# Scratch in DRAM in rows of 2304 and 3072 bytes instead of 6144 to 12288

## Chip, cores and metric

One core of a Trainium2 chip runs the whole kernel. The metric is the device time of one launch in microseconds (us). Everything is float32; matmuls of the FFN use float32r operands, split into a high and a low part.

## What is computed

A block of an adaLN-conditioned model on x of 2048 x 576: a state-space convolution (S4D) in the first half, a ReLU FFN of width 4608 in the second, each behind a layernorm that is scaled and shifted by a conditioning vector.

```python
mod = (_silu(c) @ w_mod).reshape(c.shape[0], 6, 1, -1)
sa, ca, ga, sb, cb, gb = (mod[:, i] for i in range(6))
h = _layernorm(x) * (1 + ca) + sa
# A_ref: K = 2 Re(sum_n C exp(A dt pos)), 576 channels x 2048 taps, with a diagonal A of 128 modes
#        y = irfft(rfft(h) * rfft(K)) causal, by channel;  + h * D_skip
x = x + ga * _A_ref(h, ...)
h = _layernorm(x) * (1 + cb) + sb
x = x + gb * (maximum(h @ w1, 0) @ w2)      # w1 576 x 4608, w2 4608 x 576
```

## The kernel before

The 2048 rows are cut into four blocks of 512 (NB). A block's convolution gives its x2 and the transposed h for the FFN; the FFN of a block takes 36 steps (NF), one for each 128 columns of w1.

**Before the FFN.** The class `KGen` computes the convolution's taps as products of factors: `W2` (2 x 32 per channel) and `W1` (16 x 2 per channel), 128 modes on the partitions, in six groups of 96 channels. For the first block the products are made at once (L71 in a helper). The factors are needed again for the other blocks' taps, so `sines` stores W2 (L328), and `save` W1 (L342), to DRAM tiles `W2d` and `W1d`, through SP's queue. One partition's line is 12288 B in W2d and 6144 B in W1d, contiguous in SBUF and in DRAM.

**The FFN** (`ffn`) runs over g = 0..143, 36 steps a block. A step loads w1 and w2 (tiles `r`), ScalarE rounds them to the high part `w` (L1246, L1256). In block 0, VectorE also computes the low part (L1249, L1259, L1260), and SP stores it to `L1d` and `L2d` (L1348); in the other three blocks SP loads it back (L1239, L1263) instead. `first` makes 14 matmuls into `hps` (L1273), `second` 14 into `acc` (L1299). The w tiles have two buffers, so a load is issued when the matmuls two steps back are done. All these transfers, about 1.2 MB a step in lines of 2304 and 2560 B, go through SP's hardware queue (q1).

**Beside the FFN** of block s runs a generator (`gens`) that prepares block s + 1. `step` draws from it at fixed points of the loop. In block 0 it is `rest` (taps of the later blocks from W1d, Zd and W2d: loads at L449 to L451, rotations on VectorE at L459 to L465, small matmuls at L490, stores `kd` at L431) and then `conv(1)`; in block 1 `finish(0)`, the remaining taps and `conv(2)`; in block 2 `finish(1)` and `conv(3)`; in block 3 `finish(2)`. The convolution works on spectra of 4 x 2 x 288 numbers for each of 128 frequencies: U of h, K of the taps, R of the taps before the split. `save` (L806) and `load` (L802) keep them in DRAM tiles `Ud`, `Kd`, `Rd`, one line of 9216 B for each partition; `product` (L972) loads a K and a U for each earlier block and multiplies them on VectorE (L994 to L1000). `conv` also loads its block of x (L909), again in lines of 9216 B. All these transfers go through POOL's software queue (q0).

The Tile framework orders instructions within an engine at build time and places the waits; what `keep_in_program_order` (class `Kept`) marks stays as written. Each engine runs its instructions in order.

Of the kernel before, what the change touches and what calls it, by code (L numbers as in the profile page):

```python
# [10 lines left out]
F32 = mybir.dt.float32  # L11
# [7 lines left out]
P = 128  # L19
# [8 lines left out]
H = 48  # L28
NH = 12
PC = 288  # L30
# [19 lines left out]
class KGen:  # L50
# [256 lines left out]
    def first(self, setup, mod):  # L307

        nc, k = self.nc, self.k
        self.W1, self.Z, self.E, self.F = {}, {}, {}, {}
        W2s, ke, ps = {}, None, {}

        def sines(g):
            E, F = self.E.pop(g), self.F.pop(g)
            W2 = W2s[g] = [
                self.pw.tile([P, 2, 32, H], F32, tag="W2", bufs=5, name=f"W2_{2 * g + u}")
                for u in range(2)  # L320
            ]
            ends = self.half_values(g, W2, E[2:4], F[0], True)
            yield
            self.half_values(g, W2, E[0:2], F[1], False)
            for out, a, b, op in ends:
                self.v(out, a, b, op)
            for u in range(2):
                nc.sync.dma_start(out=k.W2d[2 * g + u], in_=W2[u].rearrange("p r b c -> p (r b c)"))  # L328
            self.moduli = self.powers(g, E[4], F[2])
            zs = self.Z[g][1]  # L330
            for u in range(2):
                nc.sync.dma_start(out=k.Zd[2 * g + u], in_=zs[:, :, :, u * H : u * H + H])

        def rows(g):
            qs = slice(24 * (g % 3), 24 * (g % 3) + 24)
            self.act(ke[:, :, qs], ps[g].rearrange("p q a -> p a q"), AF.Copy)
            if g % 3 == 2:
                self.store(0, g // 3, ke.rearrange("p a q -> p (a q)"), nc.sync)

        def save(g):  # L340
            for u in range(2):
                nc.sync.dma_start(  # L342
                    out=k.W1d[2 * g + u], in_=self.W1[g][:, u].rearrange("p a r c -> p (a r c)")
                )

        def end():
            save(NG - 1)
            rows(NG - 1)

        def run(*gens):  # L350
            for x in gens:
                for _ in x:
                    pass

        def some(x, n):
            for _ in range(n):
                next(x, None)

        next(setup)
        next(mod)  # L360
        early = k.early(self)
        next(early)
        turns = self.turns(0)
        next(turns)
        next(setup)
        some(turns, 2)
        next(setup)
        run(turns, self.exps(0))
        next(mod)
        next(setup)  # L370
        next(mod)
        values = sines(0)
        next(values)
        next(mod)
        run(values)
        late = iter(())
        for g in range(NG):
            self.moduli()
            if g + 1 == NG:
                next(early)  # L380
            double = [
                self.doubling(g, i, u)
                for i, u in (
                    (0, slice(0, 2)), (1, slice(0, 2)), (2, slice(0, 1)), (2, slice(1, 2)),
                    (3, slice(0, 1)), (3, slice(1, 2)),
                )
            ]
            if g + 1 < NG:
                for i, _ in enumerate(self.exps(g + 1)):
                    some(late, 2 - i % 2)  # L390
            run(*double[:2])
            next(mod, None)
            run(double[2])
            if 0 < g < 5:
                next(early)
            if g + 1 < NG:
                turns = self.turns(g + 1)
                for _ in range(2):
                    next(turns)
                    some(late, 2)  # L400
                next(double[3])
                next(turns)
                run(late, turns, double[3])
            else:
                run(late, double[3])
            if g + 1 == NG:
                next(early)
            if g > 0:
                rows(g - 1)
            run(*double[4:])  # L410
            if g + 1 < NG:
                save(g)
            if g % 3 == 0:
                ke = self.pc.tile([P, 16, 72], F32, tag="ke", bufs=1, name=f"ke_{g}")
            ps[g] = self.ps.tile([P, 512], F32, tag="kps", name=f"kps_{g}")[:, :384].rearrange(
                "p (q a) -> p q a", a=16
            )
            a, late = (self.products(ps[g], self.W1[g], W2s[g][u], u) for u in range(2))
            if g + 2 == NG:
                self.kt0 = self.pw.tile([P, 16, 72], F32, tag="W2", bufs=5, name="kt_0")  # L420
                k.load_kt(self.kt0, 0, 0, nc.sync)
            if g + 1 < NG:
                run(a, sines(g + 1))
            if g + 2 == NG:
                next(early)
        return a, late, end
# [8 lines left out]
    def rest(self, psum, hs, blocks):  # L435


        nc, k = self.nc, self.k
        v = nc.vector.tensor_tensor
        na = 16 * len(blocks)  # L440
        with ExitStack() as ctx:
            pt = k.pool(ctx, f"kr{hs[0]}{blocks[0]}", side="right")

            def load(h):
                W2 = pt.tile([P, 2, 32, H], F32, tag="W2", bufs=2, name=f"W2r_{h}")
                W0 = pt.tile([P, 16, 2, H], F32, tag="W0", bufs=2, name=f"W0_{h}")
                Z = pt.tile([P, 2, 2, H], F32, tag="Z", bufs=2, name=f"Zr_{h}")
                d = nc.gpsimd.dma_start
                d(out=W0.rearrange("p a r c -> p (a r c)"), in_=k.W1d[h])  # L449
                d(out=Z.rearrange("p i r c -> p (i r c)"), in_=k.Zd[h])  # L450
                d(out=W2.rearrange("p r b c -> p (r b c)"), in_=k.W2d[h])  # L451
                return W2, W0, Z

            def rot(out, X, Z, i):
# [60 lines left out]
            for h in hs:  # L515
                W2, W0, Z = nxt
# [5 lines left out]
            yield from prev  # L522


def spread(a, b, n):

    for i, w in enumerate(a):
        yield w
        if i % n == n - 1:
            yield next(b, 0.0)  # L530
    yield from b


class Body:
# [3 lines left out]
    def build(self):  # L538
        nc, tc, I = self.nc, self.tc, self.I
        with ExitStack() as ctx:  # L540
            dr = ctx.enter_context(tc.tile_pool(name="dram", bufs=1, space=DRAM))
            self.kd = [[dr.tile([P, 16 * 72], F32, name=f"kd_{s}_{p}") for p in range(2)] for s in range(NB)]
            self.W2d = [dr.tile([P, 64 * H], F32, name=f"W2d_{h}") for h in range(NH)]
            self.W1d = [dr.tile([P, 32 * H], F32, name=f"W1d_{h}") for h in range(NH)]
            self.Zd = [dr.tile([P, 4 * H], F32, name=f"Zd_{h}") for h in range(NH)]
            spec = lambda n, m: [
                [dr.tile([P, 8 * PC], F32, name=f"{n}_{i}_{p}") for p in range(2)] for i in range(m)
            ]
            self.Ud, self.Rd, self.Kd = spec("Ud", 4), spec("Rd", 3), spec("Kd", 3)
            self.md = {n: dr.tile([1, D], F32, name=f"md_{n}") for n in ("ca", "sa", "gb")}  # L550
            self.cst = ctx.enter_context(tc.tile_pool(name="cst", bufs=1))
            self.L1d = [dr.tile([P, 640], F32, name=f"L1d_{f}") for f in range(NF)]
            self.L2d = [dr.tile([P, D], F32, name=f"L2d_{f}") for f in range(NF)]
            self.consts()
            self.x2, self.xT, self.ended = {}, {}, -1
            self.dsk = self.cst.tile([1, D], F32, name="dsk")
            nc.gpsimd.dma_start(out=self.dsk, in_=I["dsk"].unsqueeze(0))
            self.sm = self.pool(ctx, "sm")
            self.x2p = [self.pool(ctx, "x2a")]
            kg = KGen(self)  # L560
            with ExitStack() as c2:
                kg.open(c2)
                setup = kg.setup(I)
                hooks = dict(zip(("first", "late", "rows"), kg.first(setup, self.mod(kg))))
            self.main(ctx, kg, hooks)
# [233 lines left out]

    def load(self, src, name):  # L800
        t = self.spec(name)
        self.nc.gpsimd.dma_start(out=t.rearrange("p a b c -> p (a b c)"), in_=src)  # L802
        return t

    def save(self, dst, t, eng=None):
        (eng or self.nc.gpsimd).dma_start(out=dst, in_=t.rearrange("p a b c -> p (a b c)"))  # L806

    def transform(self, src, fc, Z, kept=False):

# [91 lines left out]
    def conv(self, s):  # L901

        nc = self.nc
        v = self.vec.tensor_tensor
        xp = self.xp[s % 2]
        if s:
            x2 = self.x2p[s % 2].tile([P, 4, D], F32, tag="x2", bufs=1, name=f"x2_{s}")
            self.x2[s] = x2
            nc.gpsimd.dma_start(  # L909
                out=x2,  # L910
                in_=self.I["x"][s * 512 : (s + 1) * 512, :].rearrange("(m n) d -> m n d", n=4),
            )
        else:
            x2, h = self.x2[0], self.h0
            self.fcKn, self.gcn = (
# [579 lines left out]
```

## Time and profile before

| | |
|---|---|
| median of 3 runs | 1414.14 us (1412.53 to 1420.44) |
| the profiled execution | 1418.65 us, span 1416.8 us |
| mean granted TensorE clock | 0.938 |
| TensorE matmul / weight load busy | 1263.9 us (89%) / 996.0 us (70%) |
| VectorE / ScalarE / GpSimd busy | 891.7 us (63%) / 495.4 us (35%) / 180.1 us (13%) |
| q1, SP's queue | 102260 packets, 222.09 MB, 47.9% of 16 engines |
| q0, POOL's queue | 17952 packets, 123.08 MB, 22.9% of 16 engines |
| first FFN matmul of the four blocks | near 229, 610, 913 and 1175 us |

"Busy" is the time in which an engine executes; the ends of matmuls are modelled, so a matmul that waits can look long. The chain of waits is followed back from the last instruction, at each step to what released it. A packet is what one of 16 DMA engines moves at a time; the DMA view gives packets, bytes and engine share by queue, and for each kind of transfer the time from issue to landing.

### The profile page before, as it was taken

The numbers are of one execution on the slowest core, as the hardware profiler recorded it, in microseconds if no ns is written. First come the engines' busy times: TensorE is split into PE (matmuls) and PEld (weight loads), VectorE is DVE, ScalarE is ACT, GpSimd is POOL, SyncE is SP. The second block draws the span as 40 slices with busy tenths as digits, with TensorE's granted clock in tenths as the row PEclk, the third lists the DMA queues.
The fourth block names the chain that finished last, engine by engine and source line by source line (L and its number), as shares of the span: only waits on it lengthen the run. The fifth ranks groups of instructions, "written<-read, shape, count | busy, mean of one in ns | idle before, by whom it ended". The sixth has DMA issues, their size and how long they took to land.

```text
span 1416.8 us, 26161 instructions
## 1 busy us (share of the span) xinstructions
PE 1263.9 (89%) x10720; PEld 996.0 (70%) x10720; DVE 891.7 (63%) x1324; ACT 495.4 (35%) x863; POOL 180.1 (13%) x277
## 2 busy tenths in 40 slices
PE   4665687999988987788999998999999999999997
PEld 2444555777867765566777786777887878888886
DVE  5899967999574776958835779463889432101102
ACT  4688323122221431161224322633322253323321
POOL 0667521000110100011010110010000000000000
PEclk9577777999999998899999999999999999999999
DMA  8658865867696767569777988585989657666662
GB/s 255 246 193 313 315 224 181 288 214 256 239 374 228 256 223 280 167 253 346 282 243 252 339 295 293 159 282 152 375 294 350 201 153 228 194 201 195 195 198 98
DMA packets 120845, 348.21 MB, mean 246 GB/s; under 512 B 23949, under 2 KB 24245, under 8 KB 109717
## 3 DMA queue, kind: packets, MB, share of 16 engines
q1 hardware_dynamic: 102260, 222.09, 47.9%
q0 software_dynamic: 17952, 123.08, 22.9%
q8 instruction: 84, 1.38, 0.4%
q10 hardware_dynamic: 512, 1.38, 0.3%
q14 instruction: 37, 0.30, 0.1%
HBM read 262.73 MB, written 83.76 MB: 245 GB/s over the span
## 4 chain that ended last, share of the span: by engine, by line
PE 66%; DVE 8%; DMA 7%; issue 2%; ACT 1%; POOL 0%; SPq 0%; POOLq 0%; ACTq 0%; DVEq 0%
PE hps L1273 28%; PE acc L1299 28%; PE kps L490 4%; PE ps_f L815 3%; DMA w<-L2d 2%; DMA L1d<-w 2%; DMA w<-L1d 2%; PE ps_i L1021 1%; DVE T L459 1%; DVE Y L1000 1%; DVE W1r L461 1%; DMA Ud<-U 1%; DVE T L998 1%; DVE W1r L465 0%; DVE w L1249 0%
## 5 line engine op out<-in xcount | busy, mean ns | idle before, releaser
L1273 PE MATMUL hps<-xh,w 128*128 128x512 f32 x1152 | 396.4, 404 | 0.0
L1299 PE MATMUL acc<-w,hh 128*128 128x512 f32 x1152 | 370.5, 403 | 6.6 <-DMA w<-L2d 6.2
L1279 DVE SCALAR_TENSOR_TENSOR hl<-hps,hh 128x512 fp32r<-128x512 f32 x144 | 99.1, 688 | 326.5 <-ACT hh L1278 326.2
L1299 PEld LDWEIGHTS acc<-w,hh 128*128 128x128 f32 x1152 | 217.3, 190 | 56.8 <-DMA w<-L2d 7.5
L1273 PEld LDWEIGHTS hps<-xh,w 128*128 128x128 f32 x1152 | 220.7, 192 | 48.6 <-ACT xh L1116 0.2
L1299 PE MATMUL acc<-w,hl 128*128 128x512 f32 x576 | 228.3, 409 | 13.2 <-DVE hl L1279 13.2
L1273 PE MATMUL hps<-xl,w 128*128 128x512 f32 x576 | 235.1, 408 | 1.6 <-DVE xl L47 1.6
L1278 ACT ACTIVATE hh<-hps 128x512 fp32r<-128x512 f32 x144 | 86.0, 597 | 366.0 <-PE hps L1273 364.2
L1256 ACT ACTIVATE w<-r 128x576 fp32r<-128x576 f32 x144 | 98.8, 686 | 251.4 <-issue 175.4
L1299 PEld LDWEIGHTS acc<-w,hl 128*128 128x128 f32 x576 | 109.7, 191 | 37.5 <-DVE hl L1279 14.1
L1273 PEld LDWEIGHTS hps<-xl,w 128*128 128x128 f32 x576 | 110.9, 193 | 26.6 <-DVE xl L47 2.7
L1273 PE MATMUL hps<-xs,w 128*128 128x512 f32 x288 | 101.7, 422 | 17.8 <-DMA w<-L1d 7.2
L1246 ACT ACTIVATE w<-r 128x640 fp32r<-128x640 f32 x144 | 105.4, 732 | 34.6 <-DMA L1d<-w 34.5
L490 PEld LDWEIGHTS kps<-W1r,W2r 128*32 128x32 f32 x3456 | 68.1, 146 | 39.8 <-issue 28.2
L490 PE MATMUL kps<-W1r,W2r 128*32 128x48 f32 (+2 forms) x3456 | 78.3, 238 | 14.9 <-issue 11.5
L71 PE MATMUL kps<-W,W 128*32 128x16 f32 x2304 | 45.1, 218 | 44.2 <-POOL W L68 29.0
L71 PEld LDWEIGHTS kps<-W,W 128*32 128x32 f32 x2304 | 40.5, 150 | 55.7 <-POOL W L68 31.4
L1000 DVE TENSOR_TENSOR Y<-Y,T 128x1152 f32<-128x1152 f32 x60 | 79.4, 1350 | 0.0
L1273 PEld LDWEIGHTS hps<-xs,w 128*128 128x128 f32 x288 | 55.0, 194 | 33.4 <-DMA w<-L1d 8.9
L816 ACT ACTIVATE Z<-ps_f 128x288 f32<-128x288 f32 x120 | 48.8, 408 | 68.8 <-PE ps_f L815 67.6
L1409 POOL DMA_DIRECT2D out_dram<-x x16 | 8.7, 546 | 462.8 <-DVE x L1401 460.4
L1299 PE MATMUL acc<-hh,w 128*128 128x512 f32 x144 | 57.4, 398 | 2.5 <-DVE w L1259 1.3
(234 smaller groups left out, 1590.1 us busy)
## 6 DMA issues: line engine op xcount, KB each, us to landing
r<-in_w_dram SPq DMA_DIRECT2D x144, 320.0 KB
r<-in_w_dram SPq DMA_DIRECT2D x144, 288.0 KB, 3.2
w<-L1d SPq DMA_DIRECT2D x108, 320.0 KB, 3.7
w<-L2d SPq DMA_DIRECT2D x108, 288.0 KB
W2r<-W2d POOLq DMA_DIRECT2D x18, 1536.0 KB, 8.8
W2d<-W SPq DMA_DIRECT2D x12, 1536.0 KB, 8.6
Ua<-Ud POOLq DMA_DIRECT2D x15, 1152.0 KB, 10.2
W<-W1d POOLq DMA_DIRECT2D x18, 768.0 KB, 9.4
```

The costliest lines, as they stand in the source:

```text
L71: self.tc.keep_in_program_order(self.nc.tensor.matmul(*args, **kw))
L459: v(T.rearrange(flat), X.rearrange(flat), zi, op=ALU.mult)
L490: nc.tensor.matmul(ps[32 * dd : 32 * dd + 32, q, :], W2[:, r, :, ch], W1[:, :, r, ch], start=(r == 0), stop=(r == 1),)
L815: nc.tensor.matmul(o, fc[:, n2, c, :], src(n2), start=True, stop=True)
L816: ev = nc.scalar.activation(Z[:, n2, c], ps[:, :PC], AF.Copy)
L1000: v(y, y, T, op=op or ALU.add)
L1246: nc.scalar.activation(w[:, 0], r, AF.Copy)
L1256: nc.scalar.activation(w[:, 0:D], r, AF.Copy)
L1273: nc.tensor.matmul(ps, a, x, start=(i == 0), stop=(i == 13))
L1278: nc.scalar.activation(hh, ps, AF.Relu)
L1279: nc.vector.scalar_tensor_tensor(hl, ps, 0.0, hh, op0=ALU.max, op1=ALU.subtract)
L1299: nc.tensor.matmul(acc[i], a, x, start=(f == 0 and seen[i] == 1), stop=(f == NF - 1 and seen[i] == (3 if i < 4 else 2)),)
```

## The change

The DRAM tiles get an outermost dimension of parts: `Ud`, `Rd`, `Kd` are [4, 128, 576] instead of [128, 2304], `W2d` is [4, 128, 768] instead of [128, 3072], `W1d` [2, 128, 768] instead of [128, 1536]. The DMAs move the same bytes between the same SBUF tiles, still one DMA for a tile; the access pattern on the DRAM side has 4 (or 2) pieces for each partition. The load of x becomes four DMAs, one for each of the four rows that a partition holds. In the built program the order of instructions on TensorE, ScalarE and VectorE differs in a few places around the statistics of x (L863 to L898) and two spots of the FFN's first block; SP's order is the same, POOL has three more issues for each x.

```diff
-                nc.sync.dma_start(out=k.W2d[2 * g + u], in_=W2[u].rearrange("p r b c -> p (r b c)"))
+                parts(nc.sync, k.W2d[2 * g + u], W2[u].rearrange("p r b c -> p (r b c)"))
...
-                nc.sync.dma_start(
-                    out=k.W1d[2 * g + u], in_=self.W1[g][:, u].rearrange("p a r c -> p (a r c)")
-                )
+                parts(nc.sync, k.W1d[2 * g + u], self.W1[g][:, u].rearrange("p a r c -> p (a r c)"))
...
-                d = nc.gpsimd.dma_start
-                d(out=W0.rearrange("p a r c -> p (a r c)"), in_=k.W1d[h])
-                d(out=Z.rearrange("p i r c -> p (i r c)"), in_=k.Zd[h])
-                d(out=W2.rearrange("p r b c -> p (r b c)"), in_=k.W2d[h])
+                d = nc.gpsimd
+                parts(d, k.W1d[h], W0.rearrange("p a r c -> p (a r c)"), True)
+                d.dma_start(out=Z.rearrange("p i r c -> p (i r c)"), in_=k.Zd[h])
+                parts(d, k.W2d[h], W2.rearrange("p r b c -> p (r b c)"), True)
...
+def parts(eng, dram, tile, load=False):
+
+    n = dram.shape[0]
+    a, b = dram.rearrange("n p f -> p n f"), tile.rearrange("p (n f) -> p n f", n=n)
+    eng.dma_start(out=b if load else a, in_=a if load else b)
...
-            self.W2d = [dr.tile([P, 64 * H], F32, name=f"W2d_{h}") for h in range(NH)]
-            self.W1d = [dr.tile([P, 32 * H], F32, name=f"W1d_{h}") for h in range(NH)]
+            self.W2d = [dr.tile([4, P, 16 * H], F32, name=f"W2d_{h}") for h in range(NH)]
+            self.W1d = [dr.tile([2, P, 16 * H], F32, name=f"W1d_{h}") for h in range(NH)]
...
-                [dr.tile([P, 8 * PC], F32, name=f"{n}_{i}_{p}") for p in range(2)] for i in range(m)
+                [dr.tile([4, P, 2 * PC], F32, name=f"{n}_{i}_{p}") for p in range(2)]
+                for i in range(m)
...
-        self.nc.gpsimd.dma_start(out=t.rearrange("p a b c -> p (a b c)"), in_=src)
+        parts(self.nc.gpsimd, src, t.rearrange("p a b c -> p (a b c)"), True)
...
-        (eng or self.nc.gpsimd).dma_start(out=dst, in_=t.rearrange("p a b c -> p (a b c)"))
+        parts(eng or self.nc.gpsimd, dst, t.rearrange("p a b c -> p (a b c)"))
...
-            nc.gpsimd.dma_start(
-                out=x2,
-                in_=self.I["x"][s * 512 : (s + 1) * 512, :].rearrange("(m n) d -> m n d", n=4),
-            )
+            rows = self.I["x"][s * 512 : (s + 1) * 512, :].rearrange("(m n) d -> m n d", n=4)
+            for n2 in range(4):
+                nc.gpsimd.dma_start(out=x2[:, n2], in_=rows[:, n2])
```

## The prediction

> **What bounds the kernel now.** I read the page first, then the chain of waits in order of time, then the stretches around each DMA that stands in it. The chain reaches back to 225 us; before that the FFN has not begun.
>
> ```profile
> span 1416.8 us, 26161 instructions
> ...
> PE 66%; DVE 8%; DMA 7%; issue 2%; ACT 1%; POOL 0%; SPq 0%; POOLq 0%; ACTq 0%; DVEq 0%
> ```
>
> In order of time (start, us, what), seven DMA pieces of it and one undisturbed set of matmuls:
>
> ```profile
> 295.27 11.28 DMA L1d<-w
> ...
> 386.69 3.17 PE hps L1273 x14
> ...
> 506.81 10.19 DMA Ud<-U
> ...
> 554.10 15.81 DMA L1d<-w
> ...
> 629.00 17.10 DMA w<-L2d
> ...
> 800.19 10.13 DMA w<-L1d
> ...
> 846.38 15.61 DMA w<-L2d
> ...
> 1056.04 12.60 DMA w<-L1d
> ```
>
> The kernel is bound by TensorE: 66% of the span is matmuls in a row, and an undisturbed set of 14 takes 3.17 us (0.226 us each). But 7% of the span is a DMA that something waits for, and four of the seven long ones are loads of the low weight parts `w<-L1d` and `w<-L2d`. They are small (320 and 288 KB) and go on SP's queue. Four `w` loads sum to 55.4 us of chain; that is not the loss, because TensorE has other work between the moment the buffer is freed and the moment the load is needed. The busy times in the stretches from issue to landing tell how much (xN is the count of instructions):
>
> ```profile
> core 0: us, PE busy (x) PEld busy (x) DVE busy (x) ACT busy (x) POOL busy (x), PEclk, DMA share, GB/s
> 295.27:306.56 11.29, 9.82 (x127) 7.49 (x125) 11.29 (x13) 1.18 (x2) 0.54 (x1) 1.00 0.95 342
> 554.10:569.92 15.82, 11.86 (x43) 8.90 (x42) 4.76 (x8) 1.79 (x3) 0.00 (x0) 0.83 1.02 408
> 629.00:646.14 17.14, 11.78 (x43) 8.61 (x41) 13.59 (x12) 3.82 (x6) 1.60 (x3) 0.90 1.03 424
> 800.19:810.36 10.17, 9.71 (x44) 7.70 (x42) 10.17 (x10) 3.74 (x6) 0.00 (x0) 1.00 1.01 378
> 846.38:862.03 15.65, 10.03 (x43) 7.62 (x41) 13.48 (x13) 3.82 (x6) 0.53 (x1) 0.98 1.01 422
> 1056.04:1068.68 12.64, 10.70 (x48) 8.46 (x46) 9.74 (x10) 3.82 (x6) 1.68 (x4) 1.00 1.01 392
> ```
>
> Busy time hides a wait, since the ends of matmuls are modelled, so I count matmuls: 43 x 0.226 = 9.7 us of work in 15.65 us at 846 leaves 5.9 us lost. The same sum gives 7.4 us at 629, 0.2 at 800 and 1.7 at 1056 (48 x 0.226 = 10.9). Together 15.2 us: that is what slow `w` loads cost. In each of the four the DMA engines are full (share 1.01 to 1.03, 378 to 424 GB/s). So the loads wait for engine time, and who gets it is in the DMA view's rows by queue (packets, MB, share of 16 engines), here for 846.4 to 862 and then for 629 to 646.1:
>
> ```profile
> DMA packets 1281, 6.60 MB, mean 423 GB/s; under 512 B 144, under 2 KB 144, under 8 KB 715
> ...
> q0 software_dynamic: 635, 5.22, 79.0%
> q1 hardware_dynamic: 646, 1.38, 22.5%
> ```
>
> ```profile
> q0 software_dynamic: 746, 5.32, 74.0%
> q1 hardware_dynamic: 891, 1.92, 28.7%
> ```
>
> q0 is POOL's queue (spectra, factors, x), q1 is SP's (weights). At 846 they moved 635 and 646 packets, one for one. Of all 1281, 566 are over 8 KB: these are q0's, 5.22 MB / 566 = 9.2 KB each, one partition's line of a spectrum. The 571 between 2 and 8 KB are q1's, 1.38 MB / 571 = 2.4 KB. So engine time is dealt out by the packet, and the queue with small packets gets 22% of it.
>
> **What the change does to the packets.** The SBUF side stays as it was; each partition's line is cut into pieces of 2304 or 3072 B on the DRAM side. No row of before shows these tensors cut so. The nearest is the end of the run (1409 to 1416.8 us), where only `out_dram` moves, in rows of 2304 B:
>
> ```profile
> DMA packets 320, 1.18 MB, mean 151 GB/s; under 512 B 64, under 2 KB 64, under 8 KB 320
> ...
> out_dram<-x POOLq DMA_DIRECT2D x4, 288.0 KB, 2.8
> ```
>
> Four stores of 128 rows are 512 rows, but there are 320 packets, 64 of them tiny: 256 packets of 4608 B. POOL's queue packs two rows into one. So I take the changed packets on q0 as 4608 B (spectra and x, from 9216) and 6144 B (W2d, from 12288); W1d was 6144 B and stays. The packets halve rather than quarter. The Trainium skill (DMA: Bandwidth & Descriptors, SWDGE vs HWDGE vs iDMA) gives a packet of the software queue as 4096 B at most, preferably. By that, rows of 2304 and 3072 B would stay single; the trace's 256 packets disagree, and I go by them.
>
> **The sum, wait by wait.** If the alternation holds, the same 646 packets of q1 meet q0 packets of half the size. At 846 q0 moves 2.61 MB instead of 5.22 while the load is pending; 2.61 MB less at 423 GB/s is 6.2 us earlier, and all of the 5.9 us lost goes. At 629 the neighbour is a mixture; of the halved kind are two W2r loads (DMA view from 621 to 650 us, and the tile's own):
>
> ```profile
> W2r<-W2d POOLq DMA_DIRECT2D x2, 1536.0 KB, 16.1
> ```
>
> ```profile
> L451 POOL DMA_DIRECT2D W2r<-W2d x2: 531/534/537, 621.9 to 624.8; - x2
> ```
>
> They are in flight for a median 16.1 us from 621.9 and 624.8, so most of their 3.15 MB falls into the wait: 1.57 MB less at 424 GB/s is 3.7 of the 7.4 us. At 1056:
>
> ```profile
> DMA packets 1238, 4.94 MB, mean 392 GB/s; under 512 B 138, under 2 KB 138, under 8 KB 902
> ...
> q0 software_dynamic: 384, 3.10, 62.7%
> ```
>
> Half of 3.10 MB at 392 GB/s is 4.0 us, more than the 1.7 lost. With 0.2 at 800 the four give 5.9 + 3.7 + 1.7 + 0.2 = **11.5 us**. The bounds are 0 and 15.2.
>
> The two `L1d<-w` stores in block 0 hold up ScalarE's `w` and behind it VectorE's split (L1249), which runs in order. At 295 VectorE is busy 11.29 of 11.29 us all the same: nothing to gain. At 554 it stands idle (timeline: start, us, instruction, idle time before it and releaser; below, the DMA view from 550 to 575):
>
> ```profile
> 565.36 0.82 DVE L1249 TENSOR_TENSOR w<-r,w 128x640 fp32r<-128x640 f32 x1 [11.06 <-ACT w L1246]
> ...
> 566.47 2.62 DVE L998 TENSOR_TENSOR T<-K,Ua 128x1152 f32<-128x1152 f32 x2
> ```
>
> ```profile
> Ka<-Kd POOLq DMA_DIRECT2D x1, 1152.0 KB, 12.1
> ```
>
> The store comes sooner, but the next product needs `Ka`, which POOL issued at 552 and which lands 12.1 us later, at 564; with a smaller share for q0 it lands later still. What is late next is that load, so I credit 0, between -11.1 (Ka had been no obstacle) and +2.
>
> What q0 loses: same bytes, smaller share, just where VectorE sets the pace, from 500 to 575 us:
>
> ```profile
> q0 software_dynamic: 1328, 10.76, 39.0%
> q1 hardware_dynamic: 3787, 8.24, 32.3%
> ```
>
> Under full contention q0 has 79% of 423 GB/s, 334; with 4608 against 2400 B it has 66%, 278. 10.76 MB then take 38.7 instead of 32.2 us: +6.5 us as an upper bound. But the engines are busy 71% of this stretch, so q0 mostly runs alone; I take +1, bounds 0 and 6.5. This +1 also holds the price of smaller packets as such. The nearest row for that is 810 to 814 us, q1 by itself in packets of 2304 and 2560 B:
>
> ```profile
> DMA packets 735, 1.59 MB, mean 397 GB/s; under 512 B 84, under 2 KB 84, under 8 KB 733
> ```
>
> 397 GB/s against 423 with large packets is 6%; q0's packets stay twice as large, so less than that, in stretches where the engines are full.
>
> Issue costs. On POOL a DMA costs about the same whatever its size, unless it has many rows (groups: busy us, mean ns of one; below, a row of the waits):
>
> ```profile
> L451 POOL DMA_DIRECT2D W2r<-W2d x18 | 9.6, 531 | 145.5 <-PE kps L490 143.2 <-DMA kd<-ker 1.3 <-DMA out_dram<-x 1.0
> ...
> L1211 POOL DMA_DIRECT2D kt<-kd x6 | 7.1, 1177 | 47.2 <-PE ps_f L815 47.2
> ```
>
> ```profile
> DVE st L863 <- DMA x<-in_x_dram: 5.9, 1, 5.9
> ```
>
> `kt<-kd` has 2048 rows, W2r 128: 0.65 us for 1920 rows, so 0.13 us for the 384 added. x becomes four issues instead of one, 3 x 0.53 = 1.6 us more of POOL's queue in each of three blocks; behind it stand W0, Z and W2 loads for a later step, and ahead of its only reader (`st`) a wait of 5.9 us in block 2, which is not in the chain. Zero, at most 1.6 each. The skill's fit in the same page (Anatomy of one DMA: 2.0 us plus bytes/436e3) would price four x loads one after the other at 10.7 against 4.7 us, an estimate; the four `out_dram` stores above, 288 KB each, overlap and land in 2.8, so this is not used.
>
> On SP the stores of W2d and W1d, 24 in the first 160 us, go from 128 rows to 512 and 256. Nearest are the stores of Zd, 512 rows, and the end of that stage (one line's durations in ns, min/median/max; then SP's timeline):
>
> ```profile
> L332 SPq DMA_DIRECT2D Zd<-zs x12: 524/1029/2090, 44.6 to 146.5; - x12
> ```
>
> ```profile
> 155.91 3.28 SPq L342 DMA_DIRECT2D W1d<-W  x2
> 173.41 1.12 SPq L431 DMA_DIRECT2D kd<-ke  x2
> ```
>
> Up to 2.1 us each against 0.32. What follows on SP (Zd, kt, the late weights) is pushed back by a few us per step. The cover is SP's own wait: after the last W1d store it stands until 173.4, some 14 us. Nothing, or up to 3 us if a buffer of W2 comes free late. I take 0.
>
> Sum: -11.5 + 0 + 1 = -10.5 us. Against the profiled execution (1418.65 us with a span of 1416.8) that is 1408.1; the median of the runs, 1414.14, is 0.3% lower, and by the same ratio gives 1403.7. **I predict 1404 us.** By the skill's packet limit (rows single) 846, 800 and 1056 give the same and 629 gives 5.6: -13.4 before q0's loss.
>
> **The rivals**, times as medians.
> - *The gain is larger.* Ka is no obstacle and the 11.1 us of VectorE's idle time at 554 go as well: -21.6, 1393. For it: the store is the releaser in the chain. Against: Ka's landing at 564.
> - *No change.* q0's loss in block 0 takes its upper bound, 6.5: -11.5 + 6.5 = -5, 1409. For it: POOL's products at 506 to 517 are in the chain already. Against: most of that stretch has a queue alone.
> - *Rows stay single on q0* (the skill's limit, and the change's own words). Then q0 gets half of 423, 212 GB/s: 10.76 MB take 50.8 us, +18.6 at most in block 0 against -13.4: between -13 and +5. If q0's loss is a third of its bound, -7, 1407.
> - *Slower.* The convolution of the next block becomes what ends each of blocks 0, 1 and 2, since its spectra come late: 3 x 6.5 = 19.5, less 11.5, is +8, 1422. It decides as soon as two of three blocks end on VectorE rather than on TensorE. For it: block 0 runs at VectorE's pace already (the idle time at 554 is in the chain). Against: blocks 1 and 2 have only `w` loads of DMA in the chain.
>
> **How the numbers follow.** Forecast 0.45 (1398 to 1409, from the bounds 15.2 and the +6.5), larger gain 0.13, no change 0.14, single rows 0.08, slower 0.20. A measurement of this kernel tells about 0.5%, 7 us, from no change: 1407 to 1421. Faster: most of the forecast (0.40), 0.13 and half of the single rows, 0.57. Same: 0.05 + 0.14 + 0.04 = 0.23. Slower: 0.20. The range goes from 1389, a little below the larger gain, to 1424, a little over the slower case.
>
> **What would show it.** Right: q0's packets under 8 KB rise and its mean size falls to some 4.5 to 6 KB; in full stretches q1's share goes from 22% to about a third; `w<-L2d` and `w<-L1d` leave the long pieces of the chain or fall under 10 us there. Wrong: packets of 2304 and 3072 B on q0; `Ka`, `Ua` or `W2r` new in the chain; VectorE's waits for `Ua<-Ud` well over their present size; blocks 1 and 2 ending on VectorE.

## The result and the profile after

| | before | after |
|---|---|---|
| median of 20 runs each, on the same chip | 1415.71 us (1411.71 to 1423.29) | 1420.71 us (1416.47 to 1427.26) |
| after / before, 95% interval | | 1.0039 (1.0026 to 1.0053) |
| profiled execution, span | 1418.65 us, 1416.8 us | 1417.84 us, 1416.1 us |

The changed kernel is slower by 0.4%, about 5.5 us. I had forecast 0.7% faster. The two profiled executions do not show it in their spans: single executions of one kernel lie up to 12 us apart, so what a change costs is taken from medians, and the profiles tell where it sits.

The packets came out as I had worked them out. First the page of the profile after, by queue, and the DMA view of after from 846.4 to 862 us, which answers to the stretch of before shown above:

```profile
q1 hardware_dynamic: 108404, 222.09, 47.6%
q0 software_dynamic: 27440, 123.08, 23.7%
```

```profile
DMA packets 1968, 6.38 MB, mean 409 GB/s; under 512 B 174, under 2 KB 174, under 8 KB 1967
...
q0 software_dynamic: 985, 4.25, 68.1%
q1 hardware_dynamic: 982, 2.13, 35.4%
```

q0 needs 27440 packets where it needed 17952, for the same bytes. In the full stretch the queues again move packet for packet (985 and 982), q0's are 4.25 MB / 985 = 4.3 KB, and q1's share has risen from 22.5% to 35.4%. And the waits that I had counted did shrink. These are rows picked out of the waits of before, then of after, over the whole span (line, releaser, us in total, times, longest):

```profile
DVE T L998 <- DMA Ua<-Ud: 20.1, 7, 6.2
PE acc L1299 <- DVE hl L1279: 13.2, 2, 8.0
PE hps L1273 <- DMA w<-L1d: 7.2, 4, 2.8
PE acc L1299 <- DMA w<-L2d: 6.2, 3, 3.6
```

```profile
DVE T L1003 <- DMA Ua<-Ud: 24.4, 8, 6.5
PE acc L1304 <- DVE hl L1284: 15.7, 4, 7.2
DVE st L869 <- DMA x<-in_x_dram: 12.6, 5, 8.3
PE hps L1278 <- DMA w<-L1d: 3.0, 2, 1.8
PE acc L1304 <- DMA w<-L2d: 1.8, 2, 1.4
```

TensorE's waits for `w` fell from 13.4 to 4.8 us. But VectorE waits longer for `Ua`, TensorE longer for VectorE's `hl`, and the statistics wait 12.6 us for x instead of 5.9. The chain of waits of after, which is followed back only to 1019 us, has two DMA pieces, and neither is a weight:

```profile
1019.48 10.30 DMA Ua<-Ud
...
1058.09 10.79 DMA Ua<-Ud
```

Before, the piece at 1056.04 was `w<-L1d`. The windows show how the gain goes. These are steps 64 and 65, then 66 and 67, of before (846.19 to 880.67) and of after (843.86 to 876.16):

```profile
846.19:867.75 21.56, 15.93 (x58) 12.28 (x56) 19.20 (x18) 3.82 (x6) 0.53 (x1) 0.85 1.00 410
867.75:880.67 12.92, 12.92 (x58) 10.66 (x56) 12.92 (x13) 3.83 (x6) 0.00 (x0) 0.98 0.61 175
```

```profile
843.86:857.14 13.28, 13.15 (x57) 10.36 (x56) 9.26 (x9) 3.83 (x6) 0.75 (x1) 1.00 1.03 413
857.14:876.16 19.02, 13.85 (x57) 10.28 (x56) 18.14 (x16) 3.81 (x6) 0.00 (x0) 1.00 0.86 315
```

Steps 64 and 65, which hold the wait that I had costed, are 8.3 us shorter, more than the 5.9 us that I had promised. The next two are 6.1 us longer. In this pair of profiles that leaves 2.2 us; over more profiles (experiment 4) it leaves nothing. TensorE's longest waits in steps 60 to 71 of after all fall in steps 66 and 67:

```profile
PE acc L1304 <- DVE hl L1284: 2.6, 2, 1.6
PE acc L1304 <- DMA w<-L2d: 1.4, 1, 1.4
PE hps L1278 <- DMA w<-L1d: 1.1, 1, 1.1
```

Half of them are waits for weights again, later and shorter than before; the other half, for `hl`, is new. VectorE's timeline tells where the new half comes from (start, us, instruction, idle time before it); first before, then after:

```profile
857.81 2.63 DVE L998 TENSOR_TENSOR T<-Ka,Ua 128x1152 f32<-128x1152 f32 x2 [1.38 <-DMA Ua<-Ud]
...
864.16 0.68 DVE L1279 SCALAR_TENSOR_TENSOR hl<-hps,hh 128x512 fp32r<-128x512 f32 x1
...
872.37 0.68 DVE L1279 SCALAR_TENSOR_TENSOR hl<-hps,hh 128x512 fp32r<-128x512 f32 x1
```

```profile
858.02 2.63 DVE L1003 TENSOR_TENSOR T<-Ka,Ua 128x1152 f32<-128x1152 f32 x2 [3.64 <-DMA Ua<-Ud]
...
864.37 0.68 DVE L1284 SCALAR_TENSOR_TENSOR hl<-hps,hh 128x512 fp32r<-128x512 f32 x1
...
872.58 0.68 DVE L1284 SCALAR_TENSOR_TENSOR hl<-hps,hh 128x512 fp32r<-128x512 f32 x1
```

The product starts near 858 us in both kernels, although after was 2.3 us ahead when step 64 began. Its `Ua` was issued 1.6 us earlier in after (837.67 against 839.29) but took 20.3 us to land instead of 18.4; the `Ua` after it took 15.2 instead of 11.1. So VectorE only waits longer for it, and the two `hl` behind it come at 864 and 872 in both. TensorE, whose weights now come sooner, reaches the matmuls that need those `hl` before they are there, and stands for 1.03 and 1.57 us.

### The profile page after: what moved, and what is told of

It reads as the page before. It is cut to its first block, busy times and chain, and to the rows that moved or that the text cites. A ratio compares the mean times of both kernels' runs of the same rounds, so it can differ in the third digit from the quotient of the medians.

```text
span 1416.1 us, 26175 instructions
## 1 busy us (share of the span) xinstructions
PE 1263.7 (89%) x10720; PEld 994.5 (70%) x10720; DVE 891.5 (63%) x1324; ACT 495.4 (35%) x863; POOL 203.9 (14%) x286
## 3 DMA queue, kind: packets, MB, share of 16 engines
q0 software_dynamic: 27440, 123.08, 23.7%
q8 instruction: 84, 1.38, 0.4%
q10 hardware_dynamic: 512, 1.38, 0.3%
## 5 line engine op out<-in xcount | busy, mean ns | idle before, releaser
L1304 PEld LDWEIGHTS acc<-w,hh 128*128 128x128 f32 x1152 | 218.3, 191 | 55.6 <-DMA w<-L2d 3.6
L1251 ACT ACTIVATE w<-r 128x640 fp32r<-128x640 f32 x144 | 105.4, 732 | 34.0 <-DMA L1d<-w 33.2
L71 PEld LDWEIGHTS kps<-W,W 128*32 128x32 f32 x2304 | 40.5, 150 | 54.5 <-POOL W L68 30.9
```

Source lines behind the costliest of these rows:

```text
L71: self.tc.keep_in_program_order(self.nc.tensor.matmul(*args, **kw))
L1251: nc.scalar.activation(w[:, 0], r, AF.Copy)
L1304: nc.tensor.matmul(acc[i], a, x, start=(f == 0 and seen[i] == 1), stop=(f == NF - 1 and seen[i] == (3 if i < 4 else 2)),)
```

## The experiments

All run on one core against the kernel before on the same chip. Times of stretches are from the profiles, counted from the first `hps` matmul of one FFN step to that of another (each step has 14).

**1. The parts alone.** Spectra: `Ud`, `Rd`, `Kd` of after; factors: `W2d`, `W1d` of after; x: the four DMAs; the rest of each as before.

```diff
 # e1_spectra_only: Ud, Rd, Kd as after; in the rest
-dr.tile([4, P, 16 * H], F32, name=f"W2d_{h}")    # W1d likewise
+dr.tile([1, P, 64 * H], F32, name=f"W2d_{h}")    # and x in one DMA
 # e2_factors_only: W2d, W1d as after; spectra [1, P, 8 * PC], x in one DMA
 # e3_x_only: the kernel before, and
+for n2 in range(4):
+    nc.gpsimd.dma_start(out=x2[:, n2], in_=rows[:, n2])
 # e4_half_rows: spectra [2, P, 4 * PC], W2d [2, P, 32 * H], W1d whole, x in one DMA
```

> Only the spectra (Ud, Rd, Kd) in rows of 2304 B; factors and x as before. Theory A (what TensorE gains on its w loads, VectorE loses on the product loads, and VectorE paces the convolution): the w waits in the chain shrink, waits for Ua<-Ud grow, and the time is +2 to +5 us. Theory B (the rows' number costs: POOL's issue and the descriptors): +2 to +3 us, about half of the whole change's +5.5. Theory C (x in four DMAs costs it all): 0 or a gain of up to 5 us here. My prediction would have -6 to -9 us.

> Only the kernel factors (W2d, W1d) in rows of 3072 B. Theory A: the loads of W2 are for TensorE's small matmuls and not on VectorE's path, so 0 to -3 us (the wait near 629 us is shorter). Theory B: +2 to +3 us, with SP's stores in the first 160 us taking longer too. Theory C: 0 to -3 us. The prediction: -3.7 us.

> Only x in four DMAs of 2304 B rows. Theory A: +1 to +2 us. Theory B: 0 to +1 us (the same number of bytes, 1.6 us more of POOL's issue, three times). Theory C: +4 to +6 us, the whole of the difference, with VectorE's wait for x and TensorE's wait for kt (which is issued behind x) grown in block 2. The prediction: 0.

> Spectra in two rows of 4608 B and W2d in two rows of 6144 B, W1d and x as before: on POOL's queue the packets are as in the changed kernel (4608 and 6144 B), with half the rows. Theory A (packet size decides): as spectra and factors together in the changed kernel, +1 to +4 us. Theory B (the number of rows decides): half or less of that, 0 to +2 us, and POOL's issue of such a DMA between 0.53 and 0.75 us. Theory C: 0 or a gain.

Measured, as ratios to before: spectra 1.0028 (1.0012 to 1.0043), factors 0.9983 (0.9964 to 1.0001), x 1.0030 (1.0016 to 1.0044), half rows with x whole 1.0001 (0.9983 to 1.0020). The three parts sum to +0.28 - 0.17 + 0.30 = +0.41%, and the whole change measured +0.39%. So two different parts cost about 4 us each, and one seems to gain some 2.5 (its interval just reaches no change). The half rows, with the spectra and W2d cut but not x, come out between the two, as they should. Theory C, x alone, falls. In the traces of the kernels with the spectra or the factors alone, and of the half rows, all five engines have the instructions of before in the order of before, so there the rows alone make the difference.

**2. The kernel before once more**, for the size of chance.

> The kernel before, unchanged, timed against itself: 0 us. Its profile is a second execution of before, which all theories expect near the median of the runs, some 4 us under the first profile's 1418.65; what differs between the two profiles, stage by stage, is what one profile can't tell.

1.0007 (0.9988 to 1.0026): the interval is 0.2% to either side, so a difference of 0.1% says nothing here, and one of 0.2% little.

**3. x: the DMAs or the order?** With x in four DMAs the built program places the square roots of the statistics (`mv`, L873) earlier among ScalarE's copies of the transforms (`Z<-ps_f`, L816): of the four at the end of block 1, one comes four copies earlier and three come two copies earlier. VectorE's order of the statistics and of one `hl` moves there too, and TensorE's near 660 us (which is in block 1, not in the FFN's first block). ScalarE runs in order. Its timeline in the kernel with x alone, at the end of block 1, and then before:

```profile
938.44 0.29 ACT L873 ACTIVATE mv<-mv,eps 128x1 f32<-128x1 f32 x1 [1.64 <-DVE mv L872]
...
942.70 0.67 ACT L873 ACTIVATE mv<-mv,eps 128x1 f32<-128x1 f32 x3 [2.41 <-DVE mv L872]
...
944.92 0.41 ACT L816 ACTIVATE Z<-ps_f 128x288 f32<-128x288 f32 x1 [0.70 <-PE ps_f L815]
948.20 0.41 ACT L816 ACTIVATE Z<-ps_f 128x288 f32<-128x288 f32 x1 [2.86 <-PE ps_f L815]
```

```profile
937.42 0.40 ACT L816 ACTIVATE Z<-ps_f 128x288 f32<-128x288 f32 x1
941.52 0.85 ACT L873 ACTIVATE mv<-mv,eps 128x1 f32<-128x1 f32 x4 [3.71 <-DVE mv L872]
942.28 0.39 ACT L816 ACTIVATE Z<-ps_f 128x288 f32<-128x288 f32 x1
```

Before, the wait for `mv` comes once, with one copy behind it. With x split it comes twice with more copies behind it, and TensorE waits for the PSUM buffers that these copies empty. This row of the waits, of the kernel with x alone from 930 to 956 us, has no counterpart in before from 926 to 950:

```profile
PE ps_f L815 <- ACT Z L816: 2.7, 2, 1.9
```

Steps 72 to 75 take 35.6 us (34.6 in after) against 30.9 in every profile of a kernel with x whole, so the whole cost of x sits there. To tell the order from the DMAs I issued the same four DMAs last row first, which puts TensorE's order back, and at this place ScalarE's and VectorE's too.

```diff
-for n2 in range(4):
+for n2 in (3, 2, 1, 0):
     nc.gpsimd.dma_start(out=x2[:, n2], in_=rows[:, n2])
```

> x in four DMAs as in the changed kernel, but the part that is read first is issued last. TensorE's order is then that of before, and ScalarE's too but for two square roots in block 1. Theory A (the order costs: with the first part of x expected early, the square roots of the layernorm stand among the evictions of ps_f on ScalarE, wait there for VectorE, and TensorE waits for the evictions): the 4.4 us of x alone go, 0 +- 1.5, and block 2 starts as before. Theory B (four DMAs cost, by POOL's issue and by kt behind them): +4 us as with x alone.

0.9985 (0.9970 to 1.0000), and 30.9 us in steps 72 to 75. Four DMAs cost nothing that can be measured; the order that they led the scheduler to cost 0.3%. The same edit in the whole change:

> The changed kernel with one edit: the four DMAs of x issued from its last row to its first. If the order of instructions that the split of x brings is what costs 4 us (Theory A), this is 4 to 5 us faster than the changed kernel: 1415 to 1418, within 2 us of before, and steps 72 to 76 take 31 us again, not 34.6. If x's four DMAs cost by themselves (Theory B): as the changed kernel, +5 us.

0.9981 (0.9960 to 1.0002) of before, where the change as it was had 1.0039: the whole net loss is gone, and steps 72 to 75 take 30.9 us. That is a step of 0.58%, where the same edit on x alone had made one of 0.45% (1.0030 to 0.9985); the intervals hold the difference.

**4. Spectra: packet size or the number of rows?** Packets of 4608 B come from 2 rows of 4608 B, 4 of 2304 or 8 of 1152 per partition: the profiles of all three have the same 24608 packets on q0.

```diff
-dr.tile([4, P, 2 * PC], F32, name=f"{n}_{i}_{p}")
+dr.tile([8, P, PC], F32, name=f"{n}_{i}_{p}")     # e7; e8: [2, P, 4 * PC]
```

> Only the spectra, in eight rows of 1152 B: packets on POOL's queue of 4608 B as with four rows, but twice the rows. Theory A (the packets' size decides, since VectorE's product loads get a smaller share): +4 to +5 us as with four rows. Theory B (the rows' number decides, by POOL's issue or by the DMA engines' time for each row): +8 to +10 us, with POOL's issue near 1.0 us.

> Only the spectra, in two rows of 4608 B: packets of 4608 B again, half the rows of the changed kernel. Theory A (packet size): +4 to +5 us. Theory B (number of rows): +1 to +2 us.

8 rows 1.0033 (1.0017 to 1.0048), 4 rows 1.0028, 2 rows 1.0019 (1.0001 to 1.0037). The three intervals overlap, so the number of rows is not shown to matter, and 8 rows are far from the +8 to +10 us of Theory B. POOL's issue of a DMA is 0.2 us dearer with 512 rows than with 128 (profile after, then before, the loads of `Ua`, ns min/median/max):

```profile
L527 POOL DMA_DIRECT2D Ua<-Ud x15: 748/748/760, 502.7 to 1079.1; - x15
```

```profile
L802 POOL DMA_DIRECT2D Ua<-Ud x15: 531/531/543, 504.2 to 1079.9; - x15
```

The exchange between steps 60 to 65 and 66 to 67 is in each of the six kernels with all spectra short and all loads kept:

| steps | long rows, 7 profiles | short rows, 6 profiles |
|---|---|---|
| 60 to 65 | 49.6 to 51.5 us | 42.8 to 44.1 |
| 66, 67 | 12.7 to 12.9 | 19.0 to 20.7 |
| sum, mean | 63.2 | 63.2 |
| 92 to 95, mean | 31.3 (29.4 to 33.2) | 33.4 (30.8 to 35.0) |

So short rows neither win nor lose in steps 60 to 67. Steps 92 to 95 are 2.1 us longer with them, in the means of ranges that overlap. In the traces of before and after, TensorE's wait for `w` there (1.9 us) is gone, and waits for VectorE's `x` (2.8 us) stand in its place.

**5. What is shared: VectorE's arithmetic or DMA time?** If TensorE's gain is lost because VectorE has too much to do there, it should be kept when VectorE has less. I cut the products, with long and with short rows:

```diff
-for y, k, u, op in (
+terms = (
     (Yr, Kr, Ur, None),
 ...
-):
+)
+for y, k, u, op in terms if i == 0 or s < 2 else terms[:1]:
```

> The kernel before, rows as long as they were, but in blocks 2 and 3 each spectral product beyond the first takes one of its four multiplications only (VectorE leaves out the others and their sums, about 7.6 us of work for each product that was cut; all loads stay). It is the base line for the next run. Theory A (VectorE, with its products' loads behind it, runs beside TensorE with almost no slack): some us faster than before, 1406 to 1414, and the loss on w<-L2d in steps 60 to 66 (51 us there, against 43 with short rows) remains, since the packets are as before. Theory B (VectorE isn't what bounds): the same as before.

> A second look at the same kernel as the run ahead of it, for the spread of the stretches in its profile: steps 60 to 68 within 2 us of that run.

> As the first of these runs (products cut), with the spectra in rows of 2304 bytes, factors and x as before; on each engine the same order. Theory A: with VectorE's work out of the way the gain on the w loads is kept: steps 60 to 66 about 7 us shorter than with long rows and 66 to 68 no longer, so 4 to 8 us faster than the first run. Theory B (short rows cost by themselves, by DMA time, POOL's issues or the stores in block 0): 3 to 6 us slower than the first run, as it was with the products whole (+4.8).

With long rows both theories missed: this kernel is slower than before, 1.0053 (1.0031 to 1.0074). The cut had moved the order on every engine but SyncE, and steps 60 to 65 took 58.0 and 53.7 us in its two profiles, so it is a poor base. With short rows it is slower still, 1.0096 (1.0063 to 1.0130), some 6 us, as Theory B had it, with 54.4 us in those steps: the gain of 7 us was not kept. Less arithmetic did not help, but as the order moved with it, this says little about VectorE's arithmetic as the limit.

So I left the arithmetic whole and took traffic away: in blocks 2 and 3 the products use the taps' spectrum that is in SBUF, and 10 loads of `Ka` (1152 KB each; the expectation's 12 was miscounted) go. This edit moved the order too, VectorE's products and `hl` in steps 60 to 67 among others; the two kernels that have it are alike in order.

```diff
-Ka = Ks[p] if t == 0 else self.load(self.Kd[s - t][p], "Ka")
+Ka = Ks[p] if t == 0 or s > 1 else self.load(self.Kd[s - t][p], "Ka")
```

> The kernel before, long rows, but in blocks 2 and 3 the products use the taps' spectrum that is in SBUF instead of loading Ka (12 loads of 1152 KB less altogether, VectorE's arithmetic whole; the products are those of other taps). It is the base line for the next run. Theory A (time of the DMA engines is what is shared): steps 60 to 68 shorter than before by 3 to 6 us, since w and Ua meet less traffic. Theory C (VectorE's arithmetic bounds these steps): 60 to 68 as before, within 2 us.

> As the run ahead of it, with the spectra in rows of 2304 bytes and the same order on each engine. Theory A: with a third of the traffic gone the rows matter less: within 3 us of the long rows in all, and steps 60 to 68 the same within 2 us. Theory C: as with all loads, +4 to +5 us.

0.9940 (0.9912 to 0.9968) with long rows, 0.9972 (0.9952 to 0.9991) with short. Steps 60 to 67 take 56.2 us with long rows and 56.1 with short, against 64.0 before. With the `Ka` loads out of the way both waits, for `w` and for `hl`, are all but gone there, and the rows make no difference. What the long rows lost there was TensorE's wait for `w`, and it went with the bytes: so `w` lacked time of the DMA engines, as Theory A has it. Whether `hl` now comes in time because of the traffic or because of the moved order is not shown, and VectorE's arithmetic is not ruled out as a part of it. And the short rows still seem to cost 0.3% in this pair, 4.5 us where Theory A had at most 3 (the two intervals overlap a little). The waits of TensorE and VectorE in steps 60 to 71 say where part of it is; rows of four kernels in turn: before, spectra alone, no `Ka` long, no `Ka` short.

```profile
PE acc L1299 <- DMA w<-L2d: 3.6, 1, 3.6
PE hps L1273 <- DMA w<-L1d: 2.0, 1, 2.0
...
DVE T L998 <- DMA Ua<-Ud: 7.6, 2, 6.2
```

```profile
PE acc L1305 <- DVE hl L1285: 5.2, 2, 3.7
PE acc L1305 <- DMA w<-L2d: 0.8, 1, 0.8
...
DVE T L1004 <- DMA Ua<-Ud: 11.9, 2, 8.1
```

```profile
PE acc L1299 <- DMA w<-L2d: 0.5, 1, 0.5
...
DVE T L998 <- DMA Ua<-Ud: 2.1, 2, 1.1
```

```profile
PE ps_i L1027 <- DVE V L842: 2.0, 1, 2.0
PE ps_i L1027 <- DVE x L1032: 1.3, 2, 0.6
...
DVE T L1004 <- DMA Ua<-Ud: 5.8, 2, 4.3
```

In both pairs short rows take TensorE's wait for `w` away (5.6 to 0.8, 0.5 to 0) and add 4 us to VectorE's wait for `Ua` (7.6 to 11.9, 2.1 to 5.8), and TensorE then waits for something of VectorE's. Where there was little wait for `w` to win, the second is a net loss: without the `Ka` loads, steps 68 to 71 take 32.1 us with long rows and 35.7 with short.

**6. Which spectra?**

```diff
-dr.tile([4, P, 2 * PC], F32, name=f"{n}_{i}_{p}")
+dr.tile([q, P, 8 // q * PC], F32, name=f"{n}_{i}_{p}")    # q = 4 for Ud alone (e13), or for Rd and Kd (e14), else 1
```

> Only Ud (the spectra of h, loaded as Ua) in rows of 2304 bytes; Rd, Kd, the factors and x as before; the order on each engine as before. If the loss sits where VectorE waits for Ua<-Ud (Theory A: engine time shared between Ua and w): most of the 4.5 us, 1418 to 1421. If it sits with the spectra of the taps (Theory B: Rd and Kd): 1415 to 1417, no change.

> Only Rd and Kd (spectra of the taps) in rows of 2304 bytes, the rest as before, the order on each engine as before. Theory A: within 2 us of before, since VectorE's waits in the products are for Ua, which comes after Ka on the same queue. Theory B: 3 to 5 us slower.

`Ud` alone 1.0003 (0.9983 to 1.0023), `Rd` and `Kd` alone 0.9991 (0.9970 to 1.0013). Neither theory places the loss: each alone costs nothing that can be measured, both together 0.2 to 0.3%. Steps 60 to 67 take 61.1 us with `Ud` alone and 62.3 with `Rd` and `Kd` alone. The loss is not shown to be in one tensor.

**7. The better versions.** Factors and the reversed x together, and the factors alone again:

> The two parts that did no harm: factors in rows of 3072 bytes (alone -3 us), x in four DMAs issued from its last row to its first (alone -1 us), spectra in long rows as before. Theory A: 1411 to 1414, 2 to 5 us below the kernel before. Theory B (a few us either way are chance of the order): within 2 us of before.

> Only the factors in rows of 3072 bytes, once more: 1412 to 1414, 2 to 4 us below the kernel before, if the first measurement (0.9983) holds; within 1 us of before if it was chance.

0.9996 (0.9972 to 1.0020), and 0.9982 (0.9960 to 1.0004). The factors alone were measured twice, 0.9983 and 0.9982; taken together (half widths combined) 0.9968 to 0.9997. That is some 2.5 us below before, just outside of chance, and 0.6% below the changed kernel. Reversing x added nothing to them. No version that computes the whole is measurably faster; the whole change with x reversed (0.9981) and x reversed alone (0.9985) are as fast.

## Why the prediction was wrong

**Packets and shares: right.** POOL's queue packs rows (4.3 KB a packet where I had 4.6), the two queues alternate, and q1's share rose to a third. The rival of single rows, which the Trainium skill's limit would have given (DMA: Bandwidth & Descriptors, SWDGE vs HWDGE vs iDMA: packets of 4096 B at most, preferably), fell: no packet of 2304 B could make 4.3 KB on average.

**The sum, wait by wait: the step that failed.** I counted the bytes that q0 no longer moves under a wait as time won, as if TensorE stood alone. Those bytes are not saved but moved later, and VectorE waits for them. For the spectra I had credited -6.8 us (-5.9, -1.7 and -0.2, with +1 for q0); they cost +4.0. At 846 I credited 5.9 us and steps 64 and 65 became 8.3 us shorter. But the engines were full there (share 1.00), so what `w` gained in time `Ua` lost (20.3 us to land instead of 18.4, then 15.2 instead of 11.1), and VectorE had no slack to lose: its product was already waiting for `Ua` (1.38 us in the row above), with `hl` behind it. Steps 60 to 67 as a whole did not move, 63.2 us against 63.2. I had put the price of this into "+1 for q0" and looked for it from 500 to 575 us only; it falls in blocks 1 and 2. At 1056 the same: -1.7 us credited, and steps 92 to 95 came out 2.1 us longer in the means.

**629, -3.7 credited: half of it came.** Steps 38 to 41, which hold that wait, take 37.6 us (36.8 to 38.4) in the mean of six profiles with short factors, against 39.6 (39.2 to 40.2) in fourteen with the factors as before, 2.1 us. Steps 8 to 11 go from 39.4 to 37.0 us in the same means, with ranges that overlap; I had not counted them.

**Block 0's store of `L1d`, 0 credited: right by luck.** I gave as the reason that the next product needs `Ka`, which lands at 564. But the row that I showed reads `K` and `Ua`; the first product that reads `Ka` starts 13 us after that landing. These are rows of VectorE's timeline, two of before and one of after:

```profile
570.79 0.83 DVE L1249 TENSOR_TENSOR w<-r,w 128x640 fp32r<-128x640 f32 x1 [0.36 <-ACT w L1246]
...
577.35 2.62 DVE L998 TENSOR_TENSOR T<-Ka,Ua 128x1152 f32<-128x1152 f32 x2
```

```profile
570.50 0.82 DVE L1254 TENSOR_TENSOR w<-r,w 128x640 fp32r<-128x640 f32 x1 [3.39 <-ACT w L1251]
```

In after the idle time of 11.06 us is down to 8.66 and the product at 566.47 starts at 563.16. VectorE then waits 3.39 us for ScalarE's next `w`, and the gain is gone. TensorE's wait for ScalarE's `w` at step 33 goes from 3.9 us in before to 1.5 in after, and a wait for VectorE's `w` of 2.3 us appears at step 34. Steps 32 to 35 take 55.6 us before and 56.5 after.

**x, 0: wrong too.** I priced POOL's three more issues and the wait of `st`. I had said in the change's description that the order moves around the statistics, and then gave that move no term in the sum. It cost 0.3% by itself, 4.2 us, and undoing it undoes the net loss. Of the some 16 us between my -10.5 and the measured +5.5, about 4 are this, about 11 the spectra and 1 the factors.

**The rivals.** The slower one had the right mechanism (spectra late, TensorE waiting for VectorE), named the right signs (`Ua` new in the chain, VectorE's waits for it grown), and its time, 1422, is the nearest; but its condition, that blocks 1 and 2 end on VectorE, was not needed: waits in the middle of a block were enough here. That its time is so near is partly luck, since half of the loss is the order of x, which it did not have.

**Still open:** where the whole 0.3% of the spectra sits. Steps 92 to 95 hold about 2 us; the rest is spread over block 0, where one profile differs from another of the same kernel by as much. Nor is it settled whether it is there in full beside short factors: the whole change with x reversed measured no slower than the factors alone. An estimate suggests that it is: over 147 runs of before, a run is 0.56 us shorter for each 0.001 more of mean granted clock. With all runs brought to one clock by that, `Ud` alone costs 0.14%, `Rd` and `Kd` alone 0.06% and all spectra 0.24 to 0.37%, and the whole change with x reversed lies 0.05% below before, where its parts sum to -0.06% (spectra +0.30, factors -0.24, x reversed -0.12). It remains an estimate, because a kernel's own stalls move its clock too.

## What to carry to other kernels

Where the DMA engines were full here, a larger share for one queue moved the wait to the reader of the other: before crediting a wait, look for the next instruction of the other reader and how long it already waits. Taking bytes out of that stretch went with 0.6% less time (the order moved too); a fairer deal gained nothing. And compare the built order before and after: splitting one load into four moved the built order, and a few square roots placed two to four copies earlier on ScalarE, with VectorE's moves around them, cost as much as the rows of the spectra did.

## What the runs showed of the hardware

A stall can cost more than its length. After the 3.59 us for `w<-L2d`, the next 14 matmuls of before took 5.72 us instead of 3.17, at a granted clock of 0.50 (windows of before):

```profile
862.03:867.75 5.72, 5.72 (x14) 4.47 (x14) 5.72 (x6) 0.00 (x0) 0.00 (x0) 0.50 0.95 374
```

That is most of why steps 64 and 65 lost 8.9 us where I had counted 5.9. In after the waits of that place are split into pieces of at most 1.6 us, and the clock of both stretches is 1.00. The Trainium skill (TensorE: Matmul & The Clock Gate, What's actually happening) has TensorE fall to half rate after an idle window of about 3.4 us; the 0.50 after 3.59 us agrees. But a shorter stall was followed by nearly the same: in the kernel with x alone, after TensorE had stood for 1.93 us at 941.78, the clock was 0.53 from 944.27 to 947.51:

```profile
944.27:947.51 3.24, 3.24 (x9) 2.48 (x8) 3.24 (x5) 0.41 (x1) 0.00 (x0) 0.53 0.47 134
```

So these runs show no length below which a stall is safe, only that pieces of 1.0 to 1.6 us left the clock alone in after.
